# Replacing a dense Fourier transform by a two-stage 47x64 one, interleaved by batch with the MLP, and Sigmoid times h by one Silu

## Chip, cores and metric

The kernel runs on one core of a Trainium2 chip. The metric is the device time of one execution in microseconds (us). The kernel before takes 1736.94 us (median of 3 runs, 1736.89 to 1738.47).

The engines are called as the profile calls them: PE (matmul), PEld (PE's weight loads, which overlap with its matmuls), DVE (VectorE), ACT (ScalarE), POOL (GpSimd), SP (the queue that issues most transfers). A "step" is always one unit of the MLP: 512 tokens times one block of 128 of the 2048 hidden features.

## The reference, cut to what matters

```python
# x (8, 3008, 256), filt_r and filt_i (1505, 256), all float32
X = np.fft.rfft(x, axis=1)
Y = X * (filt_r + 1j * filt_i)[None]
y = np.fft.irfft(Y, n=3008, axis=1)         # a global filter along the sequence
t = y.reshape(24064, 256)
h = t @ w_in                                # w_in (256, 2048)
g = h * (1.0 / (1.0 + np.exp(-beta * h)))   # beta (2048,)
out = g @ w_out                             # w_out (2048, 256)
```

## The kernel before

It has two stages, one after the other. The first multiplies all eight batches by dense cosine and sine tables (1505 frequencies by 1505 folded positions), filters, and writes the spectrum to DRAM. The second reads the spectrum back and, for each third of the positions and each batch, does 48 dense inverse matmuls and then 32 MLP steps on the two mirrored halves that come out. I call that unit a group; there are 24.

```python
# forward, for each block kb of 128 frequencies (cut)
for cb in range(NCBF):
    for mm in range(NMH):                     # 12 blocks of positions
        nc.tensor.matmul(xr_ps[:Kb], lhsT=cos_tab[:pm, mm, :Kb],
                         rhs=xe_sb[:pm, mm, c0 : c0 + CB], ...)
    for mm in range(NMH):
        nc.tensor.matmul(xi_ps[:Kb], lhsT=sin_tab[:pm, mm, :Kb],
                         rhs=xo_sb[:pm, mm, c0 : c0 + CB], ...)
# ... next tables, filter on DVE, spectrum to DRAM ...

# inverse and MLP
for ncb in range(NNI):                        # 3 blocks of positions
    cos_ti, sin_ti = tabs_cur                 # tables read back from DRAM
    for bb in range(B):                       # 8 batches: one "group" each
        # ps[0..3]: four PSUM tiles, one buffer each (pool with bufs=1)
        # ... 24 matmuls of cos_ti into psA = ps[0:2], 24 of sin_ti into psB = ps[2:4] ...
        # ... yT_lo = a + b and yT_hi = reversed(a - b), on DVE ...
        for yT, tbase, jmin, jmax in blocks:  # lo and hi
            for fb in range(NFB):             # 16 steps
                hps = mpsum.tile([P, 512], F32, name="hps", tag="hps")
                for dc in range(NDC):
                    nc.tensor.matmul(hps[:, :Nn], lhsT=win_sb[...], rhs=yT[:, dc, :Nn], ...)
                sig = mpool.tile([P, 512], F32, name="sig", tag="sig")
                nc.scalar.activation(sig[:, :Nn], hps[:, :Nn], ACT.Sigmoid,
                                     scale=beta_sb[:, fb : fb + 1])
                gT = mpool.tile([P, 512], BF16, name="gT", tag="gT")
                nc.vector.tensor_tensor(gT[:, :Nn], hps[:, :Nn], sig[:, :Nn], ALU.mult)
                for tb in range(nchunk):      # 4
                    nc.tensor.matmul(ps[tb][:tw, :D], lhsT=gT[:, tb * P : tb * P + tw],
                                     rhs=wout_sb[:, fb, :], ...)
            # ... ACT copies ps[tb] to ostage, SP writes it out ...
```

The same four PSUM tiles `ps` serve the inverse transform, the accumulation of the lo half and that of the hi half, and each has one buffer. And the order of the instructions on each engine is left to a scheduler.

## Time and profile before

| stretch of the span | us | what runs |
|---|---|---|
| 0 to 520 | 520 | tables, transposes, reversal of x, 1,152 forward matmuls |
| 520 to 562 | 42 | PE idle: inverse tables are read back |
| 562 to 1736 | 1174 | 24 groups: 1,152 inverse matmuls and 768 steps |

First the page of the kernel before: busy time of each engine, then the span in 40 slices of 43.4 us, with the busy share in tenths.

```profile
span 1736.5 us, 18868 instructions
...
PE 1303.9 (75%) x7100; PEld 666.1 (38%) x7200; DVE 927.4 (53%) x1332; ACT 681.7 (39%) x1322; POOL 4.2 (0%) x19
...
PE   0032259999980268999888888899888988888886
...
PEclk9965569999995689999999999999999999999998
DMA  4178312212258200000002000000000000000000
```

PE is the busiest engine at 75%, but the share is an average over unlike stages. It does next to nothing in the first two slices and stops in the thirteenth, and even in the long second half it shows mostly 8. The busy time of chosen windows puts numbers on this (window, then busy us and count for each engine, granted clock, DMA share, GB/s):

```profile
50.00:80.00 30.00, 0.00 (x0) 0.00 (x0) 0.00 (x0) 0.00 (x0) 0.00 (x0) 1.00 0.07 24
...
520.00:562.00 42.00, 0.00 (x0) 0.00 (x0) 3.69 (x6) 0.00 (x0) 0.00 (x0) 0.52 0.88 340
562.00:1736.00 1174.00, 992.58 (x5685) 523.92 (x5760) 559.51 (x864) 579.70 (x1009) 0.00 (x0) 0.97 0.09 28
```

From 50 to 80 us nothing computes and the 16 DMA engines are 7% busy, which is what one of them would be. The first 520 us hold only about 249 us of matmul issue (1,152 x 0.216); the view of waits has PE waiting 157.1 us there for the folded positions that DVE makes from x and its reversed copy. From 520 to 562 us PE waits for a transfer. For the last stage, compare with what PE must issue. In dense stretches the timeline starts a 128x512 matmul every 0.216 us and a 128x256 one every 0.109 us. One step is 2 x 0.216 + 4 x 0.109 = 0.868 us, and the whole MLP 653 us; the inverse matmuls are about 245 us. That is 898 us in a stage of 1174, so 276 us are lost there.

Where? These are the waits between 700 and 1700 us (engine and line, what released it, us in total, times, longest):

```profile
ACT sig L409 <- PE hps L401: 348.0, 447, 7.3
PEld L419 <- DVE gT L416: 276.5, 547, 1.6
DVE gT L416 <- ACT sig L409: 207.4, 427, 1.9
```

And these are the groups of instructions from the page (busy us, mean ns, then idle time before them and its releaser). The last is the 46 us wait of PE for the inverse tables.

```profile
L409 ACT ACTIVATE sig<-hps,beta_sb 128x512 f32<-128x512 f32 (+1 forms) x768 | 498.7, 680 | 381.4 <-PE hps L401 381.1
L416 DVE TENSOR_TENSOR gT<-hps,sig 128x512 bf16<-128x512 f32 (+1 forms) x768 | 501.0, 679 | 262.7 <-ACT sig L409 233.4
...
L355 PE MATMUL ps_3236<-cos_ti,yrg_3196 128*128 128x512 bf16 x3 | 1.8, 616 | 46.5 <-DMA cos_ti<-tcos_dram 46.3
```

### The profile page before, as it was taken

Reading aid. Unit: us, or ns where it says so; the run is one execution under the profiler, and the core shown is the slowest. Engines: PE = TensorE matmul, PEld = TensorE weight load, DVE = VectorE, ACT = ScalarE, POOL = GpSimd, SP = SyncE. Lnnn points to the kernel's source line nnn. Section 1 sums busy time; section 2 is a strip of 40 time slices with the busy share of each in tenths; the row PEclk is TensorE's granted clock in tenths of the full one; section 3 lists DMA queues with packets and bytes.
Section 4 is the critical chain, followed back from the end, with each engine's and each line's share of the span. In section 5 each row is a group of like instructions: output and inputs, shape, how many; then the busy total and the mean of one; then the engine's idle time right before and its main releaser. Section 6 shows DMA issues by size and latency. Waiting matters only on the chain.

```text
span 1736.5 us, 18868 instructions
## 1 busy us (share of the span) xinstructions
PE 1303.9 (75%) x7100; PEld 666.1 (38%) x7200; DVE 927.4 (53%) x1332; ACT 681.7 (39%) x1322; POOL 4.2 (0%) x19
## 2 busy tenths in 40 slices
PE   0032259999980268999888888899888988888886
PEld 0010024444440134444444444444444544444443
DVE  6044469999990045455554554545555544444444
ACT  1000103333310045555555555555555554444444
POOL 0000000000000000000000000000000000000000
PEclk9965569999995689999999999999999999999998
DMA  4178312212258200000002000000000000000000
GB/s 148 59 246 298 126 55 97 95 58 88 85 176 321 93 23 25 25 22 19 22 25 98 25 25 25 25 25 25 25 25 19 19 23 23 21 15 23 24 24 23
DMA packets 89058, 113.64 MB, mean 65 GB/s; under 512 B 7497, under 2 KB 81923, under 8 KB 87943
## 3 DMA queue, kind: packets, MB, share of 16 engines
q1 hardware_dynamic: 56757, 67.39, 11.6%
q10 hardware_dynamic: 32209, 45.05, 7.5%
q8 instruction: 56, 0.92, 0.2%
q14 instruction: 36, 0.29, 0.1%
HBM read 66.00 MB, written 58.72 MB: 72 GB/s over the span
## 4 chain that ended last, share of the span: by engine, by line
PE 47%; DVE 17%; DMA 15%; ACT 10%; SPq 4%; issue 4%; another core or an unknown queue 2%; ACTq 0%; DVEq 0%
PE hps L401 11%; DVE gT L416 9%; ACT sig L409 8%; DMA xb<-xrev_dram 6%; PE xr_ps L208 4%; PE xi_ps L218 4%; DMA out_dram<-ostage 3%; SPq L169 3%; DMA yr_dram<-yr_stage 2%; ACT ostage L433 2%; DMA yrg_3208<-yr_dram 2%; DMA xrev_dram<-in_x_dram 1%; PE trp L143 1%; DVE yT_lo L381 1%
## 5 line engine op out<-in xcount | busy, mean ns | idle before, releaser
L409 ACT ACTIVATE sig<-hps,beta_sb 128x512 f32<-128x512 f32 (+1 forms) x768 | 498.7, 680 | 381.4 <-PE hps L401 381.1
L416 DVE TENSOR_TENSOR gT<-hps,sig 128x512 bf16<-128x512 f32 (+1 forms) x768 | 501.0, 679 | 262.7 <-ACT sig L409 233.4
L419 PEld LDWEIGHTS <-gT 128*128 128x128 bf16 (+1 forms) x3072 | 262.2, 100 | 357.7 <-DVE gT L416 309.7
L208 PE MATMUL xr_ps<-xe_sb,cos_tab 128*128 128x512 bf16 (+2 forms) x563 | 156.3, 412 | 160.3 <-DVE xe_sb L189 157.1
L401 PE MATMUL hps<-yT_lo,win_sb 128*128 128x512 bf16 (+1 forms) x741 | 216.9, 376 | 16.1 <-DVE yT_lo L381 14.8
L401 PE MATMUL hps<-yT_hi,win_sb 128*128 128x512 bf16 (+1 forms) x736 | 225.1, 375 | 1.2
L401 PEld LDWEIGHTS <-win_sb 128*128 128x128 bf16 x1536 | 150.3, 98 | 74.2 <-issue 23.3
L218 PE MATMUL xi_ps<-xo_sb,sin_tab 128*128 128x512 bf16 (+2 forms) x564 | 143.8, 394 | 7.5 <-DVE xo_sb L190 6.9
L208 PEld LDWEIGHTS <-cos_tab 128*128 128x128 bf16 (+1 forms) x576 | 58.0, 105 | 226.6 <-issue 181.4
L144 ACT ACTIVATE sstg<-trp 128x128 bf16<-128x128 bf16 x144 | 39.8, 276 | 158.9 <-PE trp L143 146.6
L189 DVE TENSOR_TENSOR xe_sb<-xa,xb 128x2048 bf16<-128x2048 f32 (+1 forms) x12 | 27.5, 2291 | 131.1 <-DMA xb<-xrev_dram 127.1
L105 ACT ACTIVATE cos_tab<-ctmp 128x1536 bf16<-128x1536 f32 x12 | 17.8, 1484 | 180.2 <-DVE ctmp L104 92.4
L218 PEld LDWEIGHTS <-sin_tab 128*128 128x128 bf16 (+1 forms) x576 | 58.0, 102 | 78.3 <-issue 20.5
L144 ACT ACTIVATE cstg<-trp 128x128 bf16<-128x128 bf16 x144 | 39.3, 273 | 45.0 <-PE trp L143 43.9
L381 DVE TENSOR_TENSOR yT_lo<-a_sb_3264,ps_3238 128x512 bf16<-128x512 f32 x1 | 0.7, 687 | 96.9 <-PE ps_3238 L371 96.9
L143 PE MATMUL trp<-ident,cos_tab 128*128 128x128 bf16 x144 | 32.7, 227 | 26.3 <-ACT cos_tab L105 23.4
L365 ACT ACTIVATE a_sb_3264<-ps_3236 128x512 f32<-128x512 f32 x1 | 0.6, 597 | 120.9 <-PE ps_3236 L355 120.9
L143 PE MATMUL trp<-ident,sin_tab 128*128 128x128 bf16 x144 | 32.8, 228 | 11.2 <-ACT sstg L144 7.2
L355 PEld LDWEIGHTS <-yrg_3196 128*128 128x128 bf16 x144 | 14.1, 98 | 65.9 <-issue 55.2
L355 PE MATMUL ps_3236<-cos_ti,yrg_3196 128*128 128x512 bf16 x3 | 1.8, 616 | 46.5 <-DMA cos_ti<-tcos_dram 46.3
L355 PEld LDWEIGHTS <-yrg_3208 128*128 128x128 bf16 x144 | 14.0, 98 | 50.2 <-DMA yrg_3208<-yr_dram 34.3
L143 PEld LDWEIGHTS <-cos_tab 128*128 128x128 bf16 x144 | 14.5, 101 | 46.3 <-ACT cos_tab L105 23.3
(1046 smaller groups left out, 1929.9 us busy)
## 6 DMA issues: line engine op xcount, KB each, us to landing
out_dram<-ostage SPq DMA_DIRECT2D x160, 128.0 KB
xa<-in_x_dram SPq DMA_DIRECT2D x6, 1024.0 KB
yr_dram<-yr_stage SPq DMA_DIRECT2D x11, 512.0 KB
yi_dram<-yi_stage ACTq DMA_DIRECT2D x11, 512.0 KB
xrev_dram<-in_x_dram ACTq DMA_DIRECT2D x5, 1024.0 KB
xrev_dram<-in_x_dram SPq DMA_DIRECT2D x5, 1024.0 KB
xb<-xrev_dram ACTq DMA_DIRECT2D x5, 1024.0 KB
xa<-in_x_dram ACTq DMA_DIRECT2D x5, 1024.0 KB
```

The costliest lines, as they stand in the source:

```text
L143: nc.tensor.transpose(trp[:], tab[:, mm, :], ident[:])
L144: nc.scalar.activation(stg[:, mm * P : (mm + 1) * P], trp[:], ACT.Copy)
L169: eng.dma_start(xrev_dram[:, m0 + j0 : m0 + j1, :], AP(x.tensor, x.offset + (S - m0 - j0) * D, [[S * D, B], [-D, j1 - j0], [1, D]],),)
L189: nc.vector.tensor_tensor(xe_sb[:pm, mm, :], xa[:pm], xb[:pm], ALU.add)
L208: nc.tensor.matmul(xr_ps[:Kb], lhsT=cos_tab[:pm, mm, :Kb], rhs=xe_sb[:pm, mm, c0 : c0 + CB], start=(mm == 0), stop=(mm == NMH - 1),)
L218: nc.tensor.matmul(xi_ps[:Kb], lhsT=sin_tab[:pm, mm, :Kb], rhs=xo_sb[:pm, mm, c0 : c0 + CB], start=(mm == 0), stop=(mm == NMH - 1),)
L355: nc.tensor.matmul(psA[dc][:, :Nn], lhsT=yr_grps[kk // KKG][:Kk, kk % KKG, col0 : col0 + P], rhs=cos_ti[:Kk, kk, :Nn], start=(kk == 0), st ...
L401: nc.tensor.matmul(hps[:, :Nn], lhsT=win_sb[:, dc, fb * P : (fb + 1) * P], rhs=yT[:, dc, :Nn], start=(dc == 0), stop=(dc == NDC - 1),)
L409: nc.scalar.activation(sig[:, :Nn], hps[:, :Nn], ACT.Sigmoid, scale=beta_sb[:, fb : fb + 1],)
L416: nc.vector.tensor_tensor(gT[:, :Nn], hps[:, :Nn], sig[:, :Nn], ALU.mult)
L419: nc.tensor.matmul(ps[tb][:tw, :D], lhsT=gT[:, tb * P : tb * P + tw], rhs=wout_sb[:, fb, :], start=(fb == 0), stop=(fb == NFB - 1),)
L433: nc.scalar.activation(ost[:tw], ps[tb][:tw, :D], ACT.Copy)
```

## The change

Three things change together.

1. The transform is split as 3008 = 47 x 64. Each batch goes through a first stage (16 matmuls of 94x512), a trip through DRAM that turns the layout, a middle stage for each of 24 residues (64-point transform, filter, 64-point inverse; the twiddle factors are inside the matrices), another trip, and a last stage (64 matmuls of 94 columns).
2. The order on PE, ACT and DVE is fixed by hand. The MLP runs over 47 blocks of 512 tokens. The second matmuls of a step are issued two steps behind the first. Transform units of batch b+1 are dealt out between the steps of batch b.
3. `Silu(beta h)` replaces `h * sigmoid(beta h)`. It is too large by the factor beta, so the rows of w_out are divided by beta at load.

The core of the diff, removed and added parts set against each other:

```diff
-    for mm in range(NMH):                    # 12 x 2 dense matmuls per tile, both ways
-        nc.tensor.matmul(xr_ps[:Kb], lhsT=cos_tab[:pm, mm, :Kb], ...)
+    def s1(i):                               # first stage, one unit of 16
+        nc.tensor.matmul(ps[:KP], lhsT=t1[:], rhs=xg[g][:, jj : jj + 2, :], ...)
+        evac(st["a1"][:, jj : jj + 2, :], ps[:KP], both and i % 2 == 1)
+        ... every fourth: a1 to DRAM; after the last: 4 reads of a2
+    def s23(i):                              # middle stage, one unit of 13
+        ... 2 matmuls with t2, p_t = ps * fr, q_t = ps * fi on DVE,
+        ... 4 matmuls with t3p, t3q, evacuation to z; d2 to DRAM, 4 reads of zz
+    def s4(i):                               # last stage, one unit of 16: 4 matmuls
+        ...
+    spans = ((0.0, 0.20), (0.32, 0.60), (0.74, 1.0))   # where in the batch before
+    ...                                                # the three stages are dealt out
-                        sig = mpool.tile([P, 512], F32, name="sig", tag="sig")
-                        nc.scalar.activation(sig[:, :Nn], hps[:, :Nn], ACT.Sigmoid, ...)
-                        nc.vector.tensor_tensor(gT[:, :Nn], hps[:, :Nn], sig[:, :Nn], ALU.mult)
+            nc.scalar.activation(
+                gT[:, :tn], hps[:, :tn], ACT.Silu, scale=beta_sb[:, fb : fb + 1]
+            )
+        for item in plan.get(s, ()):         # transform units due at this step
+            ...
+        if s >= LAG:                         # LAG = 2
+            i, fb = steps[s - LAG]
+            ... four matmuls of gT and w_out into acc (3 buffers)
+            if fb == NFB - 1:                # DVE copies acc to ost, one write of 512 KB
```

PSUM after the change: two buffers for hps, three for acc, three for the transform. Batch 0 has nothing to hide behind, so its units run first, and ACT shares its evacuations (`both`).

## The prediction

> **What bounds it now.** By the busy table in windows, up to 520 us runs the forward transform: 1,152 dense 128x512 matmuls, with tables, transposes and x reversal; from 50 to 80 us one DMA engine of 16 works (share 0.07). PE then idles to 562 us (the first inverse matmul waited 46.3 us for cos_ti). From 562 to 1736 us: inverse and MLP. In the timeline dense PE issues a 128x512 matmul every 0.216 us, a 128x256 one every 0.109 us, at granted clock 1.00. One MLP step of 512 tokens is 2 x 0.216 + 4 x 0.109 = 0.868 us; 752 steps are 653 us; 1,152 inverse matmuls about 245 us: 898 us of issue in a 1174 us stage. The loss is in the view of waits (700 to 1700 us): weight loads of gT waited 276.5 us for DVE's gT, behind sigmoid (0.688 us) and multiply (0.688 us) in series. So: PE work plus a latency chain.
>
> **What the change does.**
> - Transform: about 1.17 million streamed columns become 32,640 per batch: 16 x 0.216 + 24 x 0.109 + 48 x 0.109 + 64 x about 0.06 (weight load and 94 columns, estimate) = 15.3 us.
> - MLP: 47 blocks in fixed order, out two steps behind. I cost Silu like sigmoid, 0.688 us; the Trainium skill, "ScalarE: Activation LUTs", What ACT_TABLE_LOAD costs, gives every function the same rate. ACT needs 0.64 to 0.69 us per 0.868 us step: not binding. With two hps buffers Silu ends about 1.4 us after a pair starts; PE wants the buffer at 1.73 us.
> - DVE loses 768 multiplies (501 us), gains per batch 24 multiplies at 0.69 us and 44 evacuations. This trace has no DVE copy from PSUM; "VectorE: DVE Perf Modes", the TRN2 errata, gives 120 + N cycles at 0.96 GHz: 0.66 us for 512 (estimate). About 43 us per batch, plus 62 us of output copies. In the middle stage DVE is nearly full: about 2 us per unit against 2.4 us of PE.
> - Batches 1 to 7 hide under the MLP; only tables and batch 0 stay exposed.
>
> **Predicted sum.**
> - Setup until DVE is free for batch 0: 65 us. About 35 us of table work (0.95 and 1.75 us per 1536-element pass); about 15 MB of loads at 250 to 300 GB/s (as in 20 to 30 and 500 to 550 us), w_out last.
> - Batch 0: stage 1 about 7 us, two trips through DRAM 8 us each, middle 19 us (DVE), last stage 7 us: 50 us.
> - 752 steps: 653 us. Seven transforms: 107 us.
> - Stalls: three accumulator buffers, copied by DVE behind FFT work, 0.6 us in 40 blocks, 25 us; late a2 reads and DVE queueing, 15 us.
> - Tail: 8 us.
> Total 923 us.
>
> **What would show it.** First Silu at 100 to 140 us; Silu mean 0.66 to 0.70 us; then PE at 9 tenths or more with clock about 1.00; no single-engine DMA stretch; 0.87 us per step in the last batch; PE's waits mostly for acc (DVE ost) and, where each middle stage starts, a2; DVE busy about 420 us.
>
> **What would make it wrong.** A Silu over 0.87 us would make ACT the bound (752 times it). The a2 gather in 512-byte pieces taking over the 10 us left for it stops PE in each of seven batches. Slow setup loads (small descriptors, casting DMA from POOL) would move the first Silu beyond 150 us. If denser PE work lowers the granted clock, everything scales.
>
> Chance of faster by over 2%: 0.98; within 2%: 0.01; slower: 0.01. Predicted 923 us, 880 to 980 us.

## The result, and the profile after

The changed kernel takes 886.58 us (median of 4 runs, 882.55 to 887.63) against 1736.91 us (4 runs). The ratio is 0.510 (95% interval 0.509 to 0.511).

| part of the time | predicted, us | measured, us |
|---|---|---|
| setup, until DVE is free for batch 0 | 65 | 60 |
| batch 0 | 50 | 50 |
| 752 steps and 7 transforms of PE issue | 653 + 107 | 758 |
| stalls of PE after that | 25 + 15 | 13 |
| tail | 8 | 5 |
| sum | 923 | 886 |

I read the measured column from the timeline: DVE's first evacuation of batch 0 starts at 60.06 us, the first hps matmul at 110.00, the last copy of an accumulator at 880.47, and the span ends at 885.9. That leaves 770.5 us between the second and the third. The issue time in it is counted on the control ctl_after, the same kernel with a trace that lacks no matmul there: its 5,800 matmuls, at 0.216 us per 512 columns and 0.06 us for 94, come to 758 us. The rest, 13 us, is stalls.

The page of the changed kernel, with slices of 22.1 us:

```profile
span 885.9 us, 14752 instructions
...
PE 783.4 (88%) x5860; PEld 551.3 (62%) x5953; DVE 414.1 (47%) x691; ACT 543.2 (61%) x789; POOL 38.2 (4%) x79
...
PE   0023599999999999999999999999999999999997
...
PEclk9999799999999999999999999999999999999999
DMA  9967465517523382507524371504523152501011
```

After five slices PE stands at 9 up to the last. The first two slices (44 us) have DMA at 9, where the kernel before had 4 in its first slice of 43 us and 1 in its second. Three windows of the same profile:

```profile
20.00:40.00 20.00, 0.00 (x0) 0.00 (x0) 18.35 (x23) 6.16 (x5) 0.00 (x0) 1.00 1.08 226
...
110.00:880.00 770.00, 756.13 (x5703) 535.38 (x5795) 349.63 (x568) 517.32 (x754) 22.76 (x44) 1.00 0.37 101
...
530.00:532.00 2.00, 1.97 (x7) 1.03 (x7) 0.78 (x2) 0.69 (x1) 0.00 (x0) 0.50 0.52 135
```

From 110 to 880 us PE is busy 756 of 770 us, and neither DVE (350) nor ACT (517) is near its limit. The third window comes back below: in it the granted clock is 0.50.

The groups that answer to those before, with the copies of the accumulators:

```profile
L449 ACT ACTIVATE gT<-hps,beta_sb 128x512 bf16<-128x512 f32 x752 | 515.8, 687 | 252.6 <-PE hps L440 217.4
L474 PE MATMUL acc<-wout_sb,gT 128*128 128x256 bf16 x3008 | 456.7, 273 | 5.1 <-DVE ost L486 0.9
...
L486 DVE COPY ost<-acc 128x512 f32<-128x512 f32 x94 | 60.2, 681 | 123.1 <-PE acc L474 123.0
```

Silu costs 687 ns, as the sigmoid did (688 ns for its 128x512 form). Of the waits of PE alone from 100 us to the end these are the four longest. The first belongs to batch 0 (before 110 us); the accumulators cost 0.9 us in five waits by this view.

```profile
PE ps_570 L386 <- DMA zz<-d_320: 7.4, 1, 7.4
PE ps_5985 L324 <- DMA a_5878<-d_5606: 2.0, 1, 2.0
PE ps_974 L324 <- DMA a_879<-d_676: 1.9, 1, 1.9
PE acc L474 <- DVE ost L486: 0.9, 5, 0.2
```

The timeline of PE in the last batch, where there is no transform left to interleave, shows the bare step:

```profile
870.79 0.59 PE L440 MATMUL hps<-y,win_sb 128*128 128x512 bf16 x2
871.22 0.60 PE L474 MATMUL acc<-wout_sb,gT 128*128 128x256 bf16 x4
871.66 0.59 PE L440 MATMUL hps<-y,win_sb 128*128 128x512 bf16 x2
```

From 870.79 to 871.66 is 0.87 us: the issue time of a step and nothing else.

So the 850 us went as follows. What ran before the overlapped stage shrank from 562 to 110 us: 452. The inverse matmuls of 245 us became seven whole transforms of 105 us: 140. The losses in the second stage fell from 276 us to 13 of stalls and 5 of tail: 258. The MLP's own 653 us didn't change. This is a comparison of two traces. No run isolates the first and largest part, so it isn't shown how much of the 452 us comes from the smaller transform itself and how much from doing without the reversed copy of x and the tables' trip through DRAM.

### The profile page after: what moved, and what is told of

The parts are those of the page before. It is cut to its first block, busy times and chain, and to the rows that moved or that the text cites. A ratio compares the mean times of both kernels' runs of the same rounds, so it can differ in the third digit from the quotient of the medians. Undisturbed runs are those within 1.5% of the kernel's fastest.

```text
span 885.9 us, 14752 instructions
## 1 busy us (share of the span) xinstructions
PE 783.4 (88%) x5860; PEld 551.3 (62%) x5953; DVE 414.1 (47%) x691; ACT 543.2 (61%) x789; POOL 38.2 (4%) x79
## 4 chain that ended last, share of the span: by engine, by line
PE 77%; DMA 14%; DVE 4%; issue 2%; ACT 1%; SPq 1%; DVEq 0%; ACTq 0%
PE acc L474 34%; PE hps L440 31%; DMA fr_sb<-in_filt_r_dram 5%; DVE ost L486 2%; DMA ws<-in_moe_w_out_dram 1%; DMA d_676<-a_738 1%; DMA d_1769<-a_1985 1%; DMA d_3048<-a_3264 1%; DMA d_5606<-a_5822 1%; DVE q_t L334 1%; DMA d_319<-a_347 1%; DMA zz<-d_677 1%; DMA d_676<-a_838 1%; DMA d_319<-a_375 1%; SPq L259 1%
## 5 line engine op out<-in xcount | busy, mean ns | idle before, releaser
L449 ACT ACTIVATE gT<-hps,beta_sb 128x512 bf16<-128x512 f32 x752 | 515.8, 687 | 252.6 <-PE hps L440 217.4
L474 PE MATMUL acc<-wout_sb,gT 128*128 128x256 bf16 x3008 | 456.7, 273 | 5.1 <-DVE ost L486 0.9
L440 PE MATMUL hps<-y,win_sb 128*128 128x512 bf16 (+7 forms) x1635 | 429.6, 351 | 0.5 <-DVE y L284 0.3
L474 PEld LDWEIGHTS <-gT 128*128 128x128 bf16 x3008 | 287.2, 98 | 143.3 <-issue 6.8
L486 DVE COPY ost<-acc 128x512 f32<-128x512 f32 x94 | 60.2, 681 | 123.1 <-PE acc L474 123.0
L386 PEld LDWEIGHTS <-zz 96*128 96x128 bf16 x512 | 36.5, 102 | 35.5 <-DMA zz<-d_320 7.7
L303 PEld LDWEIGHTS <-t_129 94*96 94x96 bf16 x128 | 16.7, 132 | 58.3 <-issue 53.1
L80 POOL DMA_DIRECT2D xg<-in_x_dram x32 | 17.2, 536 | 570.2 <-PE ps_6948 L303 85.1
L349 PEld LDWEIGHTS <-t3q 128*128 128x128 bf16 x192 | 19.1, 99 | 8.7 <-issue 5.6
L349 PEld LDWEIGHTS <-t3p 128*128 128x128 bf16 x192 | 19.1, 99 | 5.7 <-DVE p_t L333 0.8
L81 POOL DMA_DIRECT2D xg<-in_x_dram x32 | 16.4, 513 | 1.6 <-DMA xg<-in_x_dram 1.6
```

The source lines that it names most:

```text
L80: nc.gpsimd.dma_start(t[:80], xv[:80, js, :])
L81: nc.gpsimd.dma_start(t[80:NP], xv[80:NP, js, :])
L303: nc.tensor.matmul(ps[:KP], lhsT=t1[:], rhs=xg[g][:, jj : jj + 2, :], start=True, stop=True)
L349: nc.tensor.matmul(ps[:, e, :], lhsT=tab[:, k0 + e, :, :].rearrange("p c k -> p (c k)"), rhs=src[:, e, :], start=first, stop=not first,)
L386: nc.tensor.matmul(ps[:, e, :NP], lhsT=zz[:, j0 % JG + e, dc * P : (dc + 1) * P], rhs=t4[:], start=True, stop=True,)
L440: nc.tensor.matmul(hps[:, pos - t0 : pos - t0 + ln], lhsT=win_sb[:, dc, fb * P : (fb + 1) * P], rhs=ys[b][:, dc, n0 : n0 + ln], start=(dc ...
```

## The experiments

My theory A: the old second stage lost its time in the chain of sigmoid and multiply; the new kernel is bound by PE's issue, thanks to the interleaving, and Silu is needed because it frees DVE. The rivals: B, the old loss lies in the order and the buffers and not in the length of the gate; and for the new kernel, that something other than PE's issue (DVE, transfers, setup) sets the time. Eleven kernels ran; all gave correct results. The kernel before was run beside them on three chips and took 1737.18 us (b_silu, a_sig, a_lump, a_dup), 1737.28 us (ctl_after, a_slack, a_wsfirst, a_early) and 1736.86 us (b_lag, a_acc2, a_best), so differences of several us between chips can be compared too.

### 1. Only Silu, in the kernel before (b_silu)

```diff
-    nc.scalar.activation(sig[:, :Nn], hps[:, :Nn], ACT.Sigmoid, scale=beta_sb[:, fb : fb + 1])
-    nc.vector.tensor_tensor(gT[:, :Nn], hps[:, :Nn], sig[:, :Nn], ALU.mult)
+    nc.scalar.activation(gT[:, :Nn], hps[:, :Nn], ACT.Silu, scale=beta_sb[:, fb : fb + 1])
-    nc.vector.tensor_copy(wout_sb[:, fb0 : fb0 + nfb, :], wout_st[:, :nfb, :])
+    # for each fb: tensor_scalar_mul by rbeta_sb[:, fb]
```

> The kernel before with one part of the change alone: one Silu in place of Sigmoid and the DVE multiply, 1/beta folded into w_out. Theory A (in the kernel before the PE time is lost to the serial chain sigmoid, multiply, out matmul): taking 0.69 us out of the chain brings the 1174 us inverse and MLP stage to between 1000 and 1080 us, total 1560 to 1650 us, and the waits of the gT weight loads fall from about 276 to under 150 us in the stretch 700 to 1700 us. Rival B (the stage is limited by how the blocks follow one another and by the shared single ps accumulators, not by the length of the gate): under 60 us gained, total above 1680 us.

Measured: 1709.69 us, ratio 0.984 (0.982 to 0.986). The chain is half as long and DVE's busy time falls from 927 to 428 us, yet the kernel gains only 27 us. That refutes A for the old stage. Counted by the starts of PE's matmuls (see experiment 2), the gaps for gT fell only from 148 to 110 us. One wait line of this run (680 to 1680 us) shows how far the old reading misled:

```profile
PEld L421 <- ACT gT L413: 203.5, 477, 1.2
```

The weight loads still wait 203.5 us for gT. The timeline shows what lies behind that; it repeats every 2.90 us for three steps (0.97 us per step where issue needs 0.87):

```profile
984.92 1.24 PE L405 MATMUL hps<-yT_lo,win_sb 128*128 128x512 bf16 x5
985.40 1.84 ACT L413 ACTIVATE gT<-hps,beta_sb 128x512 bf16<-128x512 f32 x3 [0.98 <-PE hps L405]
986.14 0.33 PEld L421 LDWEIGHTS <-gT 128*128 128x128 bf16 x4 [0.47 <-ACT gT L413]
986.14 1.19 PE L421 MATMUL ps<-wout_sb,gT 128*128 128x256 bf16 x8
...
988.30 1.84 ACT L413 ACTIVATE gT<-hps,beta_sb 128x512 bf16<-128x512 f32 x3 [1.05 <-PE hps L405]
```

PE's order puts the hps matmuls of three steps in a bundle, and the second matmuls of three steps nearly so. ACT then stands idle for about 1 us, gets three tiles at once, needs 1.84 us for them, and PE waits for ACT. Shortening the gate helps little as long as the work is bundled.

### 2. Only a fixed order with lag 2, in the kernel before (b_lag)

```diff
+    tc.manual_schedule(engines={PE, Activation, DVE})   # around the groups
-    for yT, ... in blocks:
-        for fb in range(NFB): hps; sig; gT; four matmuls of gT
+    for s in range(32 + 2):
+        if s < 32: hps; sig; gT of step s               # Sigmoid and multiply kept
+        if s >= 2: four matmuls of gT of step s - 2
```

> The kernel before with Sigmoid and multiply kept, but the order of the MLP fixed as in the changed kernel: in each group of 32 steps the out matmuls run two steps behind, across both blocks, on PE, ACT and DVE. Theory A (after b_silu: the waits for gT came from the order of PE, which put the out matmuls of three steps right behind one another, and not from the length of the gate): the waits for gT nearly vanish, a group takes about 41 us instead of 45.2, total 1620 to 1670 us. Rival B (both the order and the 1.4 us gate are needed to hide it, two steps of 0.868 us are too short for sigmoid and multiply): above 1700 us, with the gT waits still over 100 us.

Measured: 1697.41 us, ratio 0.978 (0.976 to 0.979). This lies between the two expectations and satisfies neither. PE's own waits from 700 to 1690 us tell why:

```profile
PE ps L431 <- ACT ostage L447: 35.8, 44, 1.9
PE ps L431 <- DVE gT L422: 24.2, 68, 0.6
PE hps L407 <- DVE yT_lo L383: 18.5, 44, 0.6
```

To compare with the kernel before, every gap between starts beyond the issue time was summed over PE's timeline from 560 us on, by what released it. This counts more than the view of waits, which begins a wait at the modelled end of the matmul before: a 128x256 matmul is shown 0.273 us long, but they start 0.109 us apart. (The two traces lack about 75 of 5,760 matmuls each; gaps that nothing released are left out.) The gaps for gT fell from 148 to 39 us. But those for the four tiles `ps` (PE waits until ACT has copied them out) rose from 29 to 82 us, those for the spectrum read from DRAM from 36 to 48, and those for yT from 19 to 28. So 74 of the 109 us that the order gained were lost again at the next limits, above all at the single-buffered `ps` at every change of half and group. A full group took 45.75 us before and takes 43.55 and 45.2 by turns here, 44.3 on average, where issue alone is 48 x 0.216 + 32 x 0.868 = 38.1. With Silu alone (b_silu) it took 44.2.

The run also shows what the PEld line is worth. Weight loads of gT still wait 185 us by the view of waits, where PE itself loses 39.

### 3. The changed kernel with Sigmoid and multiply (a_sig)

```diff
-    nc.scalar.activation(gT[:, :tn], hps[:, :tn], ACT.Silu, scale=...)
+    nc.scalar.activation(sig[:, :tn], hps[:, :tn], ACT.Sigmoid, scale=...)
+    nc.vector.tensor_tensor(gT[:, :tn], hps[:, :tn], sig[:, :tn], ALU.mult)
     # and w_out copied without the division by beta
```

> The changed kernel with one part undone: Sigmoid to an f32 tile and the multiply on DVE again, the rest as changed. Theory A (Silu matters here because the multiply lengthens the time that each of two hps buffers is held and loads DVE): hps held for 0.63 + 0.69 + 0.69 + gaps, about 2.1 us against the 1.73 us of two steps, so a step of about 1.05 us and DVE full in the middle stages: 1020 to 1130 us, DVE busy about 930 us. Rival B (PE stays the bound, the multiply hides): below 920 us.

Measured: 1051.29 us, ratio 0.605, as A expected. DVE's busy time goes from 414 to 870 us, 83% of the span. PE's longest waits (112 to 1040 us):

```profile
PE acc L474 <- DVE ost L486: 51.1, 46, 1.9
PE hps L438 <- DVE gT L451: 21.4, 86, 1.1
```

PE waits for DVE at every turn of the accumulators. The waits in this view (80 us with those for q_t) are only part of the 164 us. Counted by PE's starts, the gaps sum to 182 us here and to 20 in the control, which is the whole difference: 94 us in front of hps matmuls (each of the two hps buffers is held until the multiply has read it), 59 for the accumulators and 24 for q_t. The edit of Silu alone is worth 27 us in the kernel before and 164 us here. It is the same instruction; that the difference lies in how full DVE is with other work fits these gaps, but no run varied DVE's load alone.

### 4. The changed kernel without interleaving (a_lump)

```diff
-    at = lo + int((hi - lo) * (a + (z - a) * i / (n - 1)))
+    at = hi                                  # all units of a batch at one step
-    units[b] = fft_units(b, xs.pop(b), False)
+    units[b] = fft_units(b, xs.pop(b), True) # ACT shares the evacuations
```

> The changed kernel with the interleaving undone: all units of a batch's transform are issued at one step just before its MLP begins (evacuations shared by ACT and DVE, as for batch 0). Theory A (interleaving hides everything of a transform but its 15.3 us of matmul): each batch exposes what batch 0 exposes after setup, about 50 us, in place of 15 us: seven times 35 us more, 1100 to 1170 us, with the granted clock falling in each lump. Rival B (the gain comes from the smaller transform alone, its latency is small once weights and tables are there): under 980 us.

Measured: 1146.63 us, ratio 0.660, as expected. So with the short transform and Silu in place, the interleaving is worth 259 us (1146.63 less the 887.77 of the control below). PE waits 64 us for a2 and 62 us for zz, the transfers that the other form hides, and another 64 us for evacuations by ACT. And the clock is lower where PE stops (0.887 over the whole run, 0.99 in the changed kernel). These are the two waits (100 to 1140 us), and the window of one of the stops:

```profile
PE ps L324 <- DMA a<-d: 64.0, 7, 10.4
PE ps L386 <- DMA zz<-d: 61.9, 9, 8.2
...
225.00:232.00 7.00, 3.88 (x44) 3.39 (x45) 2.56 (x5) 1.99 (x5) 0.00 (x0) 0.50 0.80 217
```

### 5. More PE work in the changed kernel (a_dup)

```diff
-    nc.tensor.matmul(ps[:KP], lhsT=t1[:], rhs=xg[g][:, jj : jj + 2, :], start=True, stop=True)
+    for _ in range(3 if b > 0 else 1):       # same result, twice overwritten
+        nc.tensor.matmul(ps[:KP], ..., start=True, stop=True)
```

> The changed kernel with each stage 1 matmul of batches 1 to 7 issued three times into the same accumulator (same result): 7 x 16 x 2 x 0.216 us = 48 us of PE work added, nothing on ACT or DVE. Theory A (after the first Silu PE issue is the bound): 48 us longer, 928 to 940 us. Rival B (the 97 to 98 per cent PE busy is the modelled ends of matmuls, and ACT, DVE or a latency sets the step): under 900 us.

Measured: 930.8 us, ratio 0.536 (0.535 to 0.537). The added issue is 7 x 32 x 0.216 = 48 us, and 43 of them came out against the control; the gaps for a2 and for the accumulators, counted by PE's starts, are 5 us smaller than there. PE's issue is what bounds the changed kernel from 110 us on.

### 6. The changed kernel again (ctl_after), and with two accumulators (a_acc2)

The control is the changed kernel as it is, on the chip on which a_slack, a_wsfirst and a_early ran as well.

> The changed kernel itself, as the control of this call: 883 to 888 us as before. The first Silu starts near 111 us; the idle time of PE after that is 2 to 8 us for the a2 reads (one wait at the start of the middle stage of most batches) and under 2 us for the output accumulators.

Measured: 887.77 us (885.35 to 889.39), ratio 0.511. Its PE waits from 112 to 886 us:

```profile
PE ps L324 <- DMA a<-d: 7.6, 5, 2.4
PE acc L474 <- DVE ost L486: 1.1, 6, 0.2
PE ps L386 <- DMA zz<-d: 0.9, 1, 0.9
```

The prediction gave 25 us to the accumulators, and 1.1 show in this view. Counted by PE's starts it is 7.0 us, in 39 gaps of about 0.18 us, beside 8.5 for a2. To see whether the third buffer is the reason, I took it away:

```diff
-    tc.tile_pool(name="opsum", bufs=3, ...)
+    tc.tile_pool(name="opsum", bufs=2, ...)
```

> The changed kernel with two output accumulators instead of three, which makes the suspected wait certain: the first out matmul of a block must wait for the first copy, the third for the second copy. Theory A (the copies are slow enough to matter, and only the third buffer hides them; my 25 us were the cost of a case that three buffers avoid): about 0.6 us in each of 47 blocks, 20 to 35 us slower than the changed kernel, 905 to 922 us, with PE waiting for ost. Rival B (the copies were never near the critical path, transform units between them give slack): below 895 us.

Measured: 909.2 us, ratio 0.523 (0.522 to 0.524): 21 us slower than the control. PE's waits (112 to 905 us):

```profile
PE acc L474 <- DVE ost L486: 18.6, 72, 0.4
```

By PE's starts the gaps for the accumulators are 34 us here, and those for a2 are 4.5 us smaller than in the control. So my 25 us were about the right price, but for two buffers. With three, PE can start the next block in the free one. In a block without transform units DVE is idle and copies at once; in a block with them, the unit that delays DVE's copy has also put matmuls in front of the one that needs the buffer. That last sentence is my reading of the timeline, not a run of its own.

### 7. Later middle and last stages (a_slack)

PE waited for a2, the data of the middle stage on their way back from DRAM. This starts the middle stage later, and makes it a little shorter:

```diff
-    spans = ((0.0, 0.20), (0.32, 0.60), (0.74, 1.0))
+    spans = ((0.0, 0.20), (0.36, 0.62), (0.76, 1.0))
```

> The middle stage of each batch starts at 36 instead of 32 per cent of the batch's steps and ends at 62 instead of 60; the last stage starts at 76 instead of 74. Theory A (of the stalls left, the a2 read through DRAM is the main one, about 8 us counted from the gaps between matmul starts, and 10 us were not enough for it): the waits for a2 vanish and the kernel is 5 to 8 us faster than the control. Rival B (those waits only shift elsewhere: DVE is too full in the shortened middle stage, and PE waits for p_t and q_t instead): within 2 us of the control, with new waits for DVE.

Measured: 876.58 us (872.1 to 877.28), ratio 0.504 (0.503 to 0.505), which is 11.2 us less than the control and more than the 5 to 8 expected. One wait of PE is left (112 to 886 us), and no a2:

```profile
PE acc L474 <- DVE ost L486: 1.3, 1, 1.3
```

The waits for a2 and zz add up to 8.5 us in the control; counted by PE's starts, all gaps together fall from 20 to 6 us. A part of them comes with the clock. After the a2 wait of 2.4 us at 528 us the granted clock was 0.57 from 530 to 534 us in the control; in this run it is 1.00 from 520 to 540. The profiled run also had a setup about 3 us shorter, which the edit does not touch (in five profiled runs with the same setup DVE's first evacuation starts between 55.0 and 60.2 us), so I don't claim the exact split.

### 8. w_out and beta loaded ahead of the filters (a_wsfirst)

In the setup DVE waited for w_out between 48 and 59 us, about 7.7 us in all. This loads beta and w_out before the filters, into four staging buffers instead of two:

```diff
+    beta_sb and the four ws loads, issued first      # wstage bufs=4
     fr_sb / fi_sb loads (32 transfers of 192 KB)
-    beta_sb and the four ws loads, in turn, bufs=2
```

> beta and w_out are loaded ahead of the filters, with four staging buffers instead of two, so that DVE has no DMA to wait for between the tables and the first evacuation. Theory A (batch 0 is held from about 44 to 60 us by the order of the loads, because w_out comes last): first evacuation of batch 0 at about 48 us instead of 60, first Silu near 99 us, total 10 to 13 us faster than the control. Rival B (the loads are limited by bandwidth, the filters land so much later that the multiplies by them hold the middle stage): less than 5 us faster.

Measured: 883.46 us, ratio 0.509 (0.508 to 0.510): 4 us less, at the edge of what these runs can tell apart (882.13 to 886.05 against 885.35 to 889.39). The size is the rival's, but not its cause: the multiplies don't wait for the filters. New waits took the place of the old one; from PE's and DVE's waits before 112 us:

```profile
PE ps L308 <- DMA xg<-in_x_dram: 6.8, 1, 6.8
...
DVE a L287 <- DMA d<-a: 8.4, 2, 7.8
```

The DMA engines are full at this time (share 1.08 from 20 to 40 us in the changed kernel). Changing the order of the loads decides who waits, not how much is to be loaded. The wait of DVE is for an a1 tile that is still being written to DRAM; it comes back below.

### 9. Stage 1 of batch 0 before the large tables (a_early)

```diff
     t1, t4 (small tables)
+    stage 1 of batch 0; then the filter loads
     t2, t3p, t3q (large tables, on DVE and ACT); w_out
-    stage 1 of batch 0
     middle and last stage of batch 0
```

(on top of a_wsfirst)

> As a_wsfirst, and stage 1 of batch 0 is issued right after its own small table, before the large tables, with the filter loads behind it. Theory A (setup is a chain of table work on DVE that batch 0's first trip through DRAM can hide under): stage 1 done by about 25 us, middle stage starts at about 55 us instead of 79, first Silu at 85 to 92 us, total 18 to 26 us faster than the control. Rival B (the first 50 us are bound by DMA, about 12 MB at 215 GB/s, and 3 MB more of scratch traffic in them delays the filters): less than 14 us faster, with the multiplies waiting for fr_sb or fi_sb.

Measured: 890.88 us (888.5 to 892.34), ratio 0.513: 3 us slower than the control, with ranges that overlap, and certainly not faster. A fails, and the wait is not the one that the rival named. DVE's waits before 115 us name the reason:

```profile
DVE a L110 <- DMA d<-a: 24.9, 1, 24.9
```

The a1 tiles have two buffers. The third a1 can only be filled when the write of the first has landed, and this write now stands in full DMA engines (share 1.06, 242 GB/s from 10 to 40 us). DVE works in order, so for 24.9 us it did not build the large tables either (it was busy 4.0 us from 10 to 40 us).

### 10. The version that the experiments point to (a_best)

a_slack and a_early together, with the in-order wait taken away by buffers: four a1 tiles. The space comes from the x tiles.

```diff
-    tc.tile_pool(name="xpool", bufs=6)
-    tc.tile_pool(name="apool", bufs=2)
+    tc.tile_pool(name="xpool", bufs=4)
+    tc.tile_pool(name="apool", bufs=4)
```

> a_slack and a_early together, with four a1 buffers instead of two (so that DVE does not stand before the third group until the first d1 write lands, which cost 24.9 us in a_early) and four x buffers instead of six (so that the next batch's x is not loaded during setup). Theory A (a_early failed through the two a1 buffers on the in-order DVE): tables done near 52 us, first Silu at 85 to 95 us, total 855 to 864 us. Rival B (the setup loads, about 12 MB moved at 215 to 240 GB/s, hold the filters and the middle stage whatever the order): first Silu after 100 us, total 868 us or more.

Measured: 857.1 us (855.42 to 857.52), ratio 0.493 (0.493 to 0.494). It beats both kernels and is 30.7 us (3.5%) under the control, though the two ran on different chips, each against its own runs of the kernel before. The first Silu starts at 90.3 us instead of 110.2 in the control; these 20 us and the 11 of a_slack make up the gain. From 20 to 40 us DVE is now busy 18.65 us, where it was busy 0 in a_early. The four x tiles were also meant to keep the x of the next batch out of the setup, but the trace has it loaded between 13.7 and 29.5 us all the same, because stage 1 of batch 0 has freed the tiles by then. That leaves the a1 tiles as what differs from a_early in the setup. What is left in PE's waits before 95 us is the setup's bandwidth and its table work:

```profile
PE ps L152 <- DMA a<-d: 26.9, 1, 26.9
...
PE ps L177 <- DVE p_t L161: 10.0, 1, 10.0
```

## Why the prediction was right, and where not

**The total and the bound of the changed kernel: right.** 886.58 us lies in the range of 880 to 980. "PE at 9 tenths or more with clock about 1.00", "0.87 us per step", "no single-engine DMA stretch" all show in the profile. The issue terms, 653 + 107 us, match the 758 us counted on the control's trace, and a_dup shows on the chip that added issue is added time.

**Silu: right.** I costed it like the sigmoid, which took 0.688 us in the trace, because the Trainium skill's page "ScalarE: Activation LUTs", section "What ACT_TABLE_LOAD costs", states one rate for every function; the trace has 687 ns for Silu. ACT is busy 517 of 770 us and does not bind. "DVE busy about 420 us" was 414.

**The mis-sized term: "Stalls: three accumulator buffers, copied by DVE behind FFT work, 0.6 us in 40 blocks, 25 us".** It measured 0.9 us in the view of PE's waits (1.1 in the control), and 7 us counted by PE's starts. I had assumed that a copy late by 0.6 us stops PE by 0.6 us. a_acc2 shows that this is the price of two buffers (18.6 us of waits, 21 us of time). This one term is 18 of the 37 us between 923 and 886. For the same reason one item of "what would show it" failed: PE's waits are not mostly for acc (7.0 us by starts in the control, a2 8.5).

**Smaller terms.** Late a2 and DVE queueing were put at 15 us; the stalls for a2 and zz sum to about 8 to 10. Setup was 60 us instead of 65 (55 to 60 over the profiled runs), the tail 5 instead of 8. All errors have the same sign.

**The wrong step: the diagnosis of the kernel before.** I wrote that the loss in its second stage is "behind sigmoid (0.688 us) and multiply (0.688 us) in series. So: PE work plus a latency chain." Halving the chain gained 27 us of 276 (b_silu). Setting the order with lag 2, which takes away most of PE's gaps for gT, gained 40 (b_lag). The loss had several causes that stand behind one another: PE's bundled order, single accumulators used for two purposes, and transfers. Removing one lets the next come out. The total was not hurt, because I costed the new kernel from issue times upward and did not subtract a gain from the old one.

**What stays open.** No run had the dense transform with all of these removed together, so I can't say how the 276 us divide. For the 6.2 us per group that b_lag still loses, the sums of gaps name accumulators, gT, yT and transfers, but none was removed singly. The forward half of the gain, 452 of 850 us, was not tested by a run of its own.

## What to carry to other kernels

A long wait in the profile names a pair of engines, not a price: read the waits of the engine that bounds (here PE, not its weight loads), and before crediting a shorter chain ask which order and which buffer will wait next. Where units are interleaved, size the buffers for the copy that they delay: one accumulator more or less was worth 21 us here, and the same Silu 27 or 164 us. Predict the new kernel from what its bounding engine must issue plus named stalls, and treat the setup apart: look at the DMA share and at in-order engines with few buffers before moving work ahead.

## What the Trainium skill lacked or had wrong

- "TensorE: Matmul & The Clock Gate", section "Why this matters for your kernels", advises no PE-idle gaps over about 3 us. Here a PE wait of 2.0 us at 527 us was followed by a granted clock of 0.50 from 530 to 532 us (and 0.57 from 530 to 534 in the control, after a wait of 2.4 us), while waits of 1.9 us near 137 us, and of 2.1 us there in the control, were not, so that their length alone doesn't tell them apart. No page gives a length below 3 us from which a stop costs clock. a_slack has no such stop and gained 11 us in all; the clock's part of that was not separated.
- "VectorE: DVE Perf Modes", the TRN2 errata, gives 120 + N cycles from PSUM to SBUF, which is 0.66 us for 512 columns. The trace has 0.681 us as the mean of one copy, and starts 0.60 us apart for two in a row. No single figure fits both; for a stream the shorter one counts, for a wait the longer one.
- "DMA: Bandwidth & Descriptors", section "Measured (HBM→SBUF, 128 partitions, SWDGE, issued from GpSimd)", has 341 GB/s for 1 MB and 425 for 16 MB. A setup that mixes casting loads with row-wise loads of 192 KB had its engines full (share 1.06 to 1.08) at 226 to 265 GB/s. A figure for such a mix is lacking. It is one of the limits of the 60 us of setup; the other is DVE's table work, busy 18.35 of the 20 us from 20 to 40.
